# Attention with two mixtures of experts: score products of both halves of a tile in a row, and gate products between the transposes and the products with v

## The chip, the cores and the metric

One core of a Trainium2 chip runs the whole kernel. The metric is the device time of one execution in microseconds (us). TensorE is called PE in the profile, VectorE DVE, ScalarE ACT, GpSimd POOL and SyncE SP.

## The reference

Attention over 4 batches, 8 heads, 576 positions and 64 columns a head, with a window of 128 positions and a distance bias; then a mixture of 8 experts (one per token, by the largest gate logit), then a dense mixture of 4 experts weighted by given probabilities.

```python
scores = scale * np.matmul(q, k.transpose(0, 1, 3, 2))
mask = (rel >= 0) & (rel < window)
scores = np.where(mask, scores + bias[None], -1000000000.0)
scores = scores - np.max(scores, axis=-1, keepdims=True)
attn = np.exp(scores)
attn = attn / (np.sum(attn, axis=-1, keepdims=True) + 1e-09)
x = np.matmul(attn, v)
...
expert_idx = np.argmax(x @ w_gate, axis=1)
out[mask] = gate_w[mask, None] * (np.maximum(x[mask] @ w1[e], 0.0) @ w2[e])
...
out += p[:, e:e + 1] * (np.maximum(x @ w1[e], 0.0) @ w2[e])
```

## The kernel before

The 2304 tokens are cut into 18 tiles of 128. A tile's queries see at most two tiles of keys (its own and the one before). Each tile is worked on in two halves of four heads; a half is a step `s`, so that tile `t` has the steps `2t` and `2t+1`, 36 in all. Only the attention part, the function `attention`, is touched by the change. The two mixtures come behind it, in `moe`.

One step of attention goes through these functions:

- `st_qk(s)`: TensorE writes the scores of a half into PSUM (tile `sc`). Two bf16 products with the identity bring the bias in (L375), then twelve products of q and k follow (L383). q and k are each split into an upper and a lower part, and the heads come in pairs, each head on 64 of the 128 rows.
- `st_max(s)`: VectorE takes the negative maximum of each row (L392, tile `nm`).
- `st_exp(s, jj)`: ScalarE takes the exponentials of one pair of heads (L400, tile `pr`), two instructions a call.
- `st_pv_t(s, jj)`: TensorE transposes the probabilities of a pair (L411, tile `pt` in PSUM), and ScalarE copies them to SBUF (L413, tile `ptr`).
- `st_pv(s)`: TensorE multiplies them with v (L426, tile `xo`). The rows of `vr` hold v, a one for the row's sum, and eight columns with the gate products of v, so that `xo` gives the gate logits too.
- `st_row(s)`: VectorE divides by the row's sum (L442 to L450); with the second half the logits of the tile are summed (L471).
- `st_vw(t)`: TensorE makes the gate products of v for one tile (L462, tile `vw`), and VectorE copies them into `vr` (L463).

The order in which the loop at L572 writes these calls is the order on each engine's queue, as each engine takes its instructions in the order of the program. Before, step `s` writes the scores of `s`, its maximum and half of its exponentials, the products with v of `s-2`, in odd steps the gate products of the tile, then the transposes of `s-1` around the other half of the exponentials of `s`. Behind these stand the chores: the splits of k and q for later tiles on VectorE (`split_k`, `split_q`), loads, in six steps the split of a weight tile (`w_split`: upper part on ScalarE at L126, lower part on VectorE at L130, one step later), and small pieces of the routing (`route_op`). At the start `busy` gives TensorE products of zeros that nobody reads (L97).

PSUM holds two buffers of `sc`, two of `pt`, and two (pool `ps_m`) that `xo`, `vw` and the routing's counts take in turn. `pr` has two buffers in SBUF.

Of the kernel before, what the change touches and what calls it, by code (L numbers as in the profile page):

```python
# [9 lines left out]
F32 = mybir.dt.float32  # L10
# [7 lines left out]
P = 128  # L18
# [29 lines left out]
def kernel(  # L48
# [44 lines left out]
    def busy(pool, tag, n):  # L93

        ps = pool.tile([P, DM], F32, tag=tag, name="idle")
        for _ in range(n):
            nc.tensor.matmul(ps, idle[:, 0:P], idle, start=True, stop=True)  # L97
# [69 lines left out]
    def attention():  # L167
        actx = ExitStack()
        with actx:
# [32 lines left out]
            def split_k(t):  # L202
                rk = raw_k.pop(t)
                c = t % NSLOT
                nc.vector.tensor_copy(out=khi[:, :, c, :], in_=rk)
                nc.vector.tensor_tensor(
                    out=klo[:, :, c, :], in0=rk, in1=khi[:, :, c, :].bitcast(F32), op=ALU.subtract
                )

            def split_q(t):  # L210
                rq = raw_q.pop(t)
                hi = qpool.tile([P, NP, P], F32R, tag="qhi", name=f"qhi{t}")
                lo = qpool.tile([P, NP, P], F32R, tag="qlo", name=f"qlo{t}")
                nc.vector.tensor_scalar(out=hi, in0=rq, scalar1=0.125, scalar2=None, op0=ALU.mult)
                nc.vector.scalar_tensor_tensor(
                    out=lo, in0=rq, scalar=0.125, in1=hi.bitcast(F32), op0=ALU.mult, op1=ALU.subtract
                )
                qs[t] = hi, lo
# [139 lines left out]
            def geom(t):  # L358
                cur, prv = t % NSLOT, (t - 1) % NSLOT
                if t in opens:  # L360
                    return [t], slice(cur, cur + 1), P
                if prv < cur:
                    return [t - 1, t], slice(prv, cur + 1, cur - prv), 0
                return [t, t - 1], slice(cur, prv + 1, prv - cur), P

            def st_qk(s):
                t, hf = divmod(s, 2)
                keys, sl, b0 = geom(t)
                w = len(keys) * P
                bias = biases[1 if t in split_tiles else 2 if t - 1 in split_tiles else 0]  # L370
                qhi, qlo = qs[t]
                ps = ps_s.tile([P, 2, 2, 2 * P], F32, tag="sc", name=f"sc{s}")
                for r in range(2):
                    h = 4 * hf + r
                    nc.tensor.matmul(  # L375
                        ps[:, r, :, 0:w], identb, bias[:, h:h + 3:2, b0:b0 + w], start=True, stop=False
                    )
                for jj in range(2):
                    j = 2 * hf + jj
                    for x, (ql, kl) in enumerate(((qhi, khi), (qhi, klo), (qlo, khi))):  # L380
                        for r in range(2):
                            rows = slice(r * D, (r + 1) * D)
                            nc.tensor.matmul(  # L383
                                ps[:, r, jj, 0:w], ql[rows, j, :], kl[rows, j, sl, :],
                                start=False, stop=(jj == 1 and x == 2),
                            )
                sc[s] = ps

            def st_max(s):
                w = len(geom(s // 2)[0]) * P  # L390
                nm = small.tile([P, 2, 2], F32, tag="nm", name=f"nm{s}")
                nc.vector.tensor_reduce(out=nm, in_=sc[s][:, :, :, 0:w], axis=AX.X, op=ALU.max, negate=True)  # L392
                pr = spool.tile([P, 2, 2, 2 * P], F32, tag="pr", name=f"pr{s}")
                prob[s] = pr, nm

            def st_exp(s, jj):
                w = len(geom(s // 2)[0]) * P
                pr, nm = prob[s]
                for r in range(2):
                    nc.scalar.activation(  # L400
                        out=pr[:, r, jj, 0:w], in_=sc[s][:, r, jj, 0:w], func=AF.Exp,
                        bias=nm[:, r, jj:jj + 1], scale=1.0,
                    )
# [12 lines left out]
            def st_pv(s):  # L416
                t, hf = divmod(s, 2)
                keys = geom(t)[0]
                nk = len(keys)
                xo = ps_m.tile([P, 4, D + 1 + E1], F32, tag="m", name=f"xo{s}")  # L420
                for jj in range(2):
                    pt = probt.pop((s, jj))
                    for r in range(2):
                        h = 4 * hf + 2 * jj + r
                        for c in range(nk):
                            nc.tensor.matmul(  # L426
                                xo[:, 2 * jj + r, :], pt[:, r, c, :], vr[:, keys[c] % NSLOT, h, :],
                                start=(c == 0), stop=(c == nk - 1),
                            )
                xos[s] = xo  # L430
# [5 lines left out]
            def st_row(s):  # L436
                t, hf = divmod(s, 2)
                xo = xos.pop(s)
                if hf == 0:
                    rowt[t] = xpool.tile([P, H, D], F32, tag="row", name=f"xrow{t}", bufs=7)  # L440
                den = small.tile([P, 4, 1], F32, tag="den", name=f"den{s}")
                nc.vector.tensor_scalar(out=den, in0=xo[:, :, D:D + 1], scalar1=1e-9, scalar2=None, op0=ALU.add)  # L442
                nc.vector.reciprocal(out=den, in_=den)
                nc.vector.tensor_tensor(
                    out=rowt[t][:, 4 * hf:4 * hf + 4, :], in0=xo[:, :, 0:D],
                    in1=den.to_broadcast([P, 4, D]), op=ALU.mult,
                )
                if hf == 0:
                    lgh[t] = xpool.tile([P, H, E1], F32, tag="lgh", name=f"lgh{t}")
                nc.vector.tensor_tensor(  # L450
                    out=lgh[t][:, 4 * hf:4 * hf + 4, :], in0=xo[:, :, D + 1:],
                    in1=den.to_broadcast([P, 4, E1]), op=ALU.mult,
                )
                if hf == 1:
                    st_logits(t)
# [111 lines left out]
            def route_op():  # L567
                todo = gates if gates and (not back or gates[0][0] < back[0][0]) else back
                if todo and next(todo[0][1], True):
                    todo.pop(0)  # L570

            for s in range(ns + 2):  # L572
                t, hf = divmod(s, 2)
                if s == 2:
                    split_k(1)
                    split_q(1)
                    busy(ps_t, "t", 3)
                if s < ns:
                    st_qk(s)
                    if s == 1:  # L580
                        busy(ps_t, "t", 4)
                    st_max(s)
                    st_exp(s, 0)
                route_op()
                if 2 <= s < ns + 2:
                    st_pv(s - 2)
                    st_row(s - 2)
                if hf == 1 and s < ns:
                    st_vw(t)
                    if t + 2 < NTT:  # L590
                        load_v(t + 2)
                route_op()
                if 1 <= s < ns + 1:
                    st_pv_t(s - 1, 0)
                if s < ns:
                    st_exp(s, 1)
                if 1 <= s < ns + 1:
                    st_pv_t(s - 1, 1)
                if s < ns:
                    if hf == 0:  # L600
                        if 2 <= t + 1 < NTT:
                            split_k(t + 1)
                        if t + 3 < NTT:
                            load(t + 3)
                    elif t + 2 < NTT:
                        split_q(t + 2)
                    if s == 1:
                        row_consts()
                    if s in (3, 5):
                        w_dma(nxt["dma"])  # L610
                    if s < E1:
                        clear_rows(s)
                    if s == 20:
                        domain_probs()
                    for _ in range(5):
                        if next(consts, True):
                            pass
                route_op()
                if late:
                    late.pop(0)()  # L620
                if s in SPLITS:
                    w_split(late)
                route_op()
            while late:
                late.pop(0)()
            for todo in (back, gates):
# [583 lines left out]
```

## Time and profile before

| What | Value |
|---|---|
| median of 3 runs | 1202.87 us (1201.73 to 1203.39) |
| the profiled execution's own time | 1197.88 us |
| its span in the trace | 1196.2 us |
| mean granted TensorE clock | 0.993 |
| PE busy | 1167.6 us, 98% |
| DVE busy | 785.6 us, 66% |
| ACT busy | 517.7 us, 43% |
| POOL busy | 94.7 us, 8% |

The shares are averages over stages with different limits. Attention takes roughly the first 176 us of the span. A busy TensorE in these tables is one whose matmul records cover the time; matmul records overlap, so the pace is read from the starts of successive records, not from their lengths.

### The profile page before, as it was taken

How to read it: one execution, taken by the hardware profiler on the slowest of the kernel's cores; microseconds unless marked ns; L12 is line 12 of the kernel's file. 1: busy time of each engine (PE TensorE's matmuls, PEld its weight loads, DVE VectorE, ACT ScalarE, POOL GpSimd, SP SyncE). 2: the span in 40 equal slices, each digit the busy share in tenths (PEclk: the TensorE clock that was granted, in tenths of full speed). 3: DMA queues.
4: the chain of work that ended last, by engine and by line, in shares of the span. 5: the costliest groups of instructions: out<-in, count | busy, mean ns of one | idle time of the engine just before them, and what ended most of it. 6: DMA issues, size and time to landing. Idle time of an engine off the chain costs nothing.

```text
span 1196.2 us, 18240 instructions
## 1 busy us (share of the span) xinstructions
PE 1167.6 (98%) x7006; PEld 1061.4 (89%) x7006; DVE 785.6 (66%) x1434; ACT 517.7 (43%) x926; POOL 94.7 (8%) x127
## 2 busy tenths in 40 slices
PE   8999998999999999999999899999999999999997
PEld 6888877999999988999999799999998899999996
DVE  6878764555565467666667876666667766666663
ACT  4565542454454344333334444443334433333331
POOL 8300110012200000000000110000000200000001
PEclk9999999999999999999999999999999999999999
DMA  9755424464574322222222222222221322222201
GB/s 315 262 163 188 142 63 155 143 200 141 159 221 149 124 72 71 71 71 71 65 63 67 89 88 69 57 69 71 71 65 58 124 72 71 71 71 71 71 19 53
DMA packets 62232, 126.67 MB, mean 106 GB/s; under 512 B 26272, under 2 KB 26272, under 8 KB 62112
## 3 DMA queue, kind: packets, MB, share of 16 engines
q1 hardware_dynamic: 58368, 114.96, 30.7%
q0 software_dynamic: 3456, 9.51, 2.1%
q8 instruction: 83, 1.36, 0.5%
q10 hardware_dynamic: 288, 0.52, 0.1%
q14 instruction: 37, 0.30, 0.1%
HBM read 109.18 MB, written 15.80 MB: 104 GB/s over the span
## 4 chain that ended last, share of the span: by engine, by line
issue 42%; PE 37%; DVE 2%; POOL 2%; ACT 1%; POOLq 0%; ACTq 0%; DVEq 0%
PE g L679 10%; PE l L1120 9%; PE y L786 8%; PE X L1026 4%; PE Z L1026 2%; POOL out_dram L1141 2%; PE y L797 1%; PE Y L1026 1%; PE xps L742 1%; DVE hlo L1062 1%; DVE x L701 0%; ACT hhi L1057 0%; DVE x L1056 0%; ACT whi L126 0%; PE g L767 0%
## 5 line engine op out<-in xcount | busy, mean ns | idle before, releaser
L130 DVE TENSOR_TENSOR wlo<-raw,whi 128x1024 fp32r<-128x1024 f32 x160 | 195.0, 1221 | 113.4 <-ACT whi L126 113.3
L1120 PE MATMUL l<-whi,hhi 128*128 128x512 f32 x576 | 225.4, 391 | 4.3 <-DVE acc L1137 4.0
L126 ACT CAST whi<-raw 128x1024 fp32r<-128x1024 f32 x160 | 168.3, 1057 | 134.1 <-DVE raw L152 104.6
L1120 PE MATMUL l<-whi,hlo 128*128 128x512 f32 x576 | 225.6, 392 | 0.0
L1120 PE MATMUL l<-wlo,hhi 128*128 128x512 f32 x576 | 225.3, 391 | 0.0
L1047 ACT COPY x<-X 128x384 f32<-128x384 f32 x138 | 65.8, 480 | 237.7 <-PE X L1026 237.7
L1137 DVE SCALAR_TENSOR_TENSOR acc<-l,ct,acc 128x512 f32<-128x512 f32 x126 | 94.3, 749 | 82.2 <-PE l L1120 82.2
L1120 PEld LDWEIGHTS l<-whi,hhi 128*128 128x128 f32 x576 | 108.6, 189 | 27.5 <-DVE acc L1137 4.8
L1120 PEld LDWEIGHTS l<-whi,hlo 128*128 128x128 f32 x576 | 108.5, 188 | 22.9 <-DVE hlo L1062 0.3
L1120 PEld LDWEIGHTS l<-wlo,hhi 128*128 128x128 f32 x576 | 108.6, 189 | 22.0
L1057 ACT ACTIVATE hhi<-x 128x384 fp32r<-128x384 f32 x144 | 74.1, 526 | 75.0 <-DVE x L1056 75.0
L1056 DVE TENSOR_TENSOR x<-Z,x 128x384 f32<-128x384 f32 x92 | 50.8, 556 | 81.9 <-ACT x L1047 72.9
L1141 POOL DMA_INDIRECT out_dram<-acc,ctok x18 | 23.0, 1276 | 842.9 <-DVE acc L1137 493.2
L1062 DVE SCALAR_TENSOR_TENSOR hlo<-x,hhi 128x384 fp32r<-128x384 f32 x144 | 77.4, 554 | 11.5 <-ACT hhi L1057 7.5
L400 ACT ACTIVATE pr<-sc,nm 128x256 f32<-128x256 f32 (+1 forms) x144 | 58.9, 464 | 52.4 <-DVE nm L392 24.6
L426 PE MATMUL xo<-vr,ptr 128*128 128x73 f32 x544 | 69.0, 279 | 0.6 <-ACT ptr L413 0.5
L786 PE MATMUL y<-hhi,whi 128*128 128x256 f32 (+2 forms) x224 | 69.5, 310 | 0.0
L786 PE MATMUL y<-hhi,wlo 128*128 128x256 f32 (+2 forms) x224 | 69.1, 308 | 0.0
L786 PE MATMUL y<-hlo,whi 128*128 128x256 f32 (+2 forms) x224 | 68.9, 308 | 0.0
L426 PEld LDWEIGHTS xo<-vr,ptr 128*128 128x128 f32 x544 | 63.7, 192 | 5.8 <-ACT ptr L413 1.3
L667 DVE SCALAR_TENSOR_TENSOR hlo<-g,hhi 128x384 fp32r<-128x384 f32 x64 | 32.7, 552 | 29.8 <-ACT hhi L666 29.5
L666 ACT ACTIVATE hhi<-g 128x384 fp32r<-128x384 f32 x64 | 28.0, 489 | 54.5 <-PE g L767 41.7
(337 smaller groups left out, 2546.4 us busy)
## 6 DMA issues: line engine op xcount, KB each, us to landing
raw<-in_w_b_dram SPq DMA_DIRECT2D x96, 512.0 KB, 3.5
raw<-in_w_a_dram SPq DMA_DIRECT2D x64, 512.0 KB, 4.1
xs<-zrow SPq DMA_DIRECT2D x8, 768.0 KB, 6.9
row<-xs SPq DMA_DIRECT2D x7, 768.0 KB, 5.6
rk<-in_k_dram SPq DMA_DIRECT2D x18, 256.0 KB, 4.9
vr<-in_v_dram SPq DMA_DIRECT2D x18, 256.0 KB, 3.9
rv<-in_vt_dram SPq DMA_DIRECT2D x18, 256.0 KB, 3.4
rq<-in_q_dram SPq DMA_DIRECT2D x16, 256.0 KB, 5.2
```

What stands on the lines that cost most here:

```text
L126: nc.scalar.copy(out=hi, in_=src)
L130: nc.vector.tensor_tensor(out=lo, in0=src, in1=hi.bitcast(F32), op=ALU.subtract)
L400: nc.scalar.activation(out=pr[:, r, jj, 0:w], in_=sc[s][:, r, jj, 0:w], func=AF.Exp, bias=nm[:, r, jj:jj + 1], scale=1.0,)
L426: nc.tensor.matmul(xo[:, 2 * jj + r, :], pt[:, r, c, :], vr[:, keys[c] % NSLOT, h, :], start=(c == 0), stop=(c == nk - 1),)
L679: nc.tensor.matmul(ps[:, 0:w], wl[:, c0:c0 + P], xl[dt // 2][:, dt % 2, 0:w], start=(n == 0), stop=(n == 3 * NDT - 1),)
L786: nc.tensor.matmul(acc[:, 0:w], wl[:, c0:c0 + P], hl[:, 0:w], start=(f == 0 and x == 0), stop=(f == NFT - 1 and x == 2),)
L1026: nc.tensor.matmul(ps, wl[:, c0 + kt * P:c0 + (kt + 1) * P], xl[:, kt, :], start=(start and kt == 0 and x == 0), stop=(kt == 1 and x == 2) ...
L1047: nc.scalar.copy(out=to, in_=xb[i])
L1057: nc.scalar.activation(out=hi, in_=c, func=AF.Relu)
L1062: nc.vector.scalar_tensor_tensor(out=lo, in0=c, scalar=0.0, in1=hi.bitcast(F32), op0=ALU.max, op1=ALU.subtract)
L1120: nc.tensor.matmul(acc, hl[:, ts], wl[:, c0:c0 + DM], start=(m == 0 and x == 0), stop=(m == 3 and x == 2),)
L1137: nc.vector.scalar_tensor_tensor(out=accs[g], in0=acc, scalar=pe, in1=accs[g], op0=ALU.mult, op1=ALU.add)
```

## The change

The loop runs over tiles instead of steps. For a tile, the scores of both halves are written one behind the other, each with its maximum, then all exponentials of the first half. Then come the products with v of the first half of the tile before, the transposes of its second half, the chores of the even step, all exponentials of the second half, the gate products, the products with v of the second half of the tile before, the transposes of this tile's first half, and the chores of the odd step. The buffer of `pr` is taken when the first exponential is written, not with the maximum. In the first tile the gate products stand ahead of four of the products of zeros instead of behind them.

```diff
                 nm = small.tile([P, 2, 2], F32, tag="nm", name=f"nm{s}")
                 nc.vector.tensor_reduce(out=nm, in_=sc[s][:, :, :, 0:w], axis=AX.X, op=ALU.max, negate=True)
-                pr = spool.tile([P, 2, 2, 2 * P], F32, tag="pr", name=f"pr{s}")
-                prob[s] = pr, nm
+                prob[s] = nm
 
             def st_exp(s, jj):
                 w = len(geom(s // 2)[0]) * P
+                if jj == 0:
+                    prob[s] = spool.tile([P, 2, 2, 2 * P], F32, tag="pr", name=f"pr{s}"), prob[s]
                 pr, nm = prob[s]
...
-            for s in range(ns + 2):
+            def chores(s):
                 t, hf = divmod(s, 2)
-                if s == 2:
-                    split_k(1)
-                    split_q(1)
-                    busy(ps_t, "t", 3)
-                if s < ns:
-                    st_qk(s)
-                    if s == 1:
-                        busy(ps_t, "t", 4)
-                    st_max(s)
-                    st_exp(s, 0)
-                route_op()
-                if 2 <= s < ns + 2:
-                    st_pv(s - 2)
-                    st_row(s - 2)
-                if hf == 1 and s < ns:
-                    st_vw(t)
-                    if t + 2 < NTT:
-                        load_v(t + 2)
-                route_op()
-                if 1 <= s < ns + 1:
-                    st_pv_t(s - 1, 0)
-                if s < ns:
-                    st_exp(s, 1)
-                if 1 <= s < ns + 1:
-                    st_pv_t(s - 1, 1)
...
+            for t in range(NTT + 1):
+                s = 2 * t
+                if t == 1:
+                    split_k(1)
+                    split_q(1)
+                    busy(ps_t, "t", 3)
+                if t < NTT:
+                    for n in (s, s + 1):
+                        st_qk(n)
+                        st_max(n)
+                    for jj in range(2):
+                        st_exp(s, jj)
+                route_op()
+                if t > 0:
+                    st_pv(s - 2)
+                    st_row(s - 2)
+                    route_op()
+                    for jj in range(2):
+                        st_pv_t(s - 1, jj)
+                chores(s)
+                if t < NTT:
+                    for jj in range(2):
+                        st_exp(s + 1, jj)
+                    st_vw(t)
+                    if t == 0:
+                        busy(ps_t, "t", 4)
+                route_op()
+                if t > 0:
+                    st_pv(s - 1)
+                    st_row(s - 1)
+                if t + 2 < NTT:
+                    load_v(t + 2)
+                route_op()
+                if t < NTT:
+                    for jj in range(2):
+                        st_pv_t(s, jj)
+                chores(s + 1)
```

**TensorE in tile 11** (steps 22 and 23). The numbers in the names are steps for `sc`, `xo`, `pt` and `ptr`, and tiles for `vw`. Before, the first half's scores are followed by products with v:

```order
L383 MATMUL sc22_1679<-khi_116,qlo11_1532 128x256 x2
L426 MATMUL xo20_1700<-vr_118,ptr20_0_1659 128x73 x4
L426 MATMUL xo20_1700<-vr_118,ptr20_1_1668 128x73 x4
L411 MATMUL pt21_0_1717<-ident_68,pr21_1629 128x128 x4
L411 MATMUL pt21_1_1726<-ident_68,pr21_1629 128x128 x4
L375 LDWEIGHTS identb_168
L375 MATMUL sc23_1742<-bias0_171,identb_168 128x512
```

and the second half's scores too, with the gate products behind them:

```order
L383 MATMUL sc23_1742<-khi_116,qlo11_1532 128x256 x2
L426 MATMUL xo21_1762<-vr_118,ptr21_0_1722 128x73 x4
L426 MATMUL xo21_1762<-vr_118,ptr21_1_1731 128x73 x4
L462 MATMUL vw11_1777<-wbd_189,rv11_1511 128x16 x4
L411 MATMUL pt22_0_1786<-ident_68,pr22_1696 128x128 x4
L411 MATMUL pt22_1_1795<-ident_68,pr22_1696 128x128 x4
L375 LDWEIGHTS identb_168
```

Now, behind the second half's scores of the same tile:

```order
L383 MATMUL sc23_1696<-khi_116,qlo11_1532 128x256 x2
L427 MATMUL xo20_1719<-vr_118,ptr20_0_1661 128x73 x4
L427 MATMUL xo20_1719<-vr_118,ptr20_1_1668 128x73 x4
L412 MATMUL pt21_0_1736<-ident_68,pr21_1629 128x128 x4
L412 MATMUL pt21_1_1743<-ident_68,pr21_1629 128x128 x4
L463 MATMUL vw11_1764<-wbd_189,rv11_1513 128x16 x4
L427 MATMUL xo21_1770<-vr_118,ptr21_0_1741 128x73 x4
L427 MATMUL xo21_1770<-vr_118,ptr21_1_1748 128x73 x4
L412 MATMUL pt22_0_1788<-ident_68,pr22_1713 128x128 x4
L412 MATMUL pt22_1_1795<-ident_68,pr22_1713 128x128 x4
```

The scores of step 23 have moved ahead of `xo20`, and `vw11` now stands between the transposes `pt21` and the products `xo21` that read them.

**ScalarE near the end of attention** (steps 30 to 32). Before, two exponentials stand between the copies of a step's two pairs:

```order
L400 ACTIVATE pr30_2237<-sc30_2220,nm30_2235 128x256 x2
L413 COPY ptr29_0_2263<-pt29_0_2258 128x512
L400 ACTIVATE pr30_2237<-sc30_2220,nm30_2235 128x256 x2
L413 COPY ptr29_1_2272<-pt29_1_2267 128x512
L400 ACTIVATE pr31_2307<-sc31_2290,nm31_2305 128x256 x2
L413 COPY ptr30_0_2341<-pt30_0_2336 128x512
```

Now:

```order
L401 ACTIVATE pr30_2254<-sc30_2220,nm30_2235 128x256 x4
L414 COPY ptr29_0_2282<-pt29_0_2277 128x512
L414 COPY ptr29_1_2289<-pt29_1_2284 128x512
L401 ACTIVATE pr31_2307<-sc31_2237,nm31_2252 128x256 x4
L414 COPY ptr30_0_2343<-pt30_0_2338 128x512
L414 COPY ptr30_1_2350<-pt30_1_2345 128x512
```

All four exponentials of a step now stand ahead of the first copy, and the two copies follow each other.

## Rows read from the trace of the kernel before

**Rows 1.** Busy time of each engine in one stretch, most of attention; last: PEclk, DMA share, GB/s

```profile
22.00:163.00 141.00, 139.84 (x1297) 122.33 (x1296) 112.75 (x315) 85.06 (x196) 30.00 (x50) 1.00 0.59 188
```

**Rows 2.** Waits of PE in that stretch: us in total, times, longest

```profile
PE rkp L513 <- DVE oh_all L506: 0.8, 1, 0.8
```

**Rows 3.** Timeline of PE, tile 11: start, us, line, count [idle before]

```profile
103.75 0.59 PE L375 MATMUL sc<-bias,identb 128*128 128x512 bf16 x2
...
105.19 2.01 PE L426 MATMUL xo<-vr,ptr 128*128 128x73 f32 x16
107.03 1.04 PE L411 MATMUL pt<-ident,pr 128*128 128x128 f32 x8
107.90 0.59 PE L375 MATMUL sc<-bias,identb 128*128 128x512 bf16 x2
...
109.33 2.01 PE L426 MATMUL xo<-vr,ptr 128*128 128x73 f32 x16
111.17 1.01 PE L462 MATMUL vw<-wbd,rv 128*128 128x16 f32 x8
112.03 1.07 PE L411 MATMUL pt<-ident,pr 128*128 128x128 f32 x8
112.94 0.59 PE L375 MATMUL sc<-bias,identb 128*128 128x512 bf16 x2
```

**Rows 4.** Timeline of PE, the last five of the sixteen products from 105.19

```profile
106.47 0.72 PE L426 MATMUL xo<-vr,ptr 128*128 128x73 f32 x5
```

**Rows 5.** Timeline of DVE, tiles 11 and 12

```profile
107.98 0.18 DVE L450 TENSOR_TENSOR lgh<-xo,den 128x32 f32<-128x32 f32 x1
...
109.20 1.22 DVE L130 TENSOR_TENSOR wlo<-raw,whi 128x1024 fp32r<-128x1024 f32 x1
...
112.74 0.42 DVE L214 TENSOR_SCALAR qhi<-rq 128x512 fp32r<-128x512 f32 x1
113.19 0.69 DVE L215 SCALAR_TENSOR_TENSOR qlo<-rq,qhi 128x512 fp32r<-128x512 f32 x1
114.48 1.23 DVE L392 TENSOR_REDUCE nm<-sc 128x4 f32<-128x1024 f32 x1 [0.60 <-PE sc L383]
```

**Rows 6.** Timeline of ACT, tiles 11 and 12

```profile
112.70 0.58 ACT L413 COPY ptr<-pt 128x512 f32<-128x512 f32 x1 [0.22 <-PE pt L411]
...
115.80 0.47 ACT L400 ACTIVATE pr<-sc,nm 128x256 f32<-128x256 f32 x1 [1.30 <-DVE nm L392]
```

**Rows 7.** Timeline of PE, the end of attention

```profile
169.89 2.33 PE L426 MATMUL xo<-vr,ptr 128*128 128x73 f32 x16 [0.24 <-ACT ptr L413]
172.06 1.04 PE L411 MATMUL pt<-ident,pr 128*128 128x128 f32 x8
```

**Rows 8.** Timeline of ACT, the end of attention

```profile
169.26 0.58 ACT L413 COPY ptr<-pt 128x512 f32<-128x512 f32 x1 [1.10 <-PE pt L411]
169.74 0.84 ACT L400 ACTIVATE pr<-sc,nm 128x256 f32<-128x256 f32 x2
170.46 0.60 ACT L413 COPY ptr<-pt 128x512 f32<-128x512 f32 x1
...
172.75 1.07 ACT L413 COPY ptr<-pt 128x512 f32<-128x512 f32 x2 [1.58 <-PE pt L411]
```

**Rows 9.** Timeline of DVE, the start, steps 1 and 2

```profile
10.50 0.23 DVE L463 COPY vr<-vw 128x64 f32<-128x64 f32 x1 [1.07 <-PE vw L462]
10.80 0.43 DVE L214 TENSOR_SCALAR qhi<-rq 128x512 fp32r<-128x512 f32 x1
```

**Rows 10.** Loads of q issued from 6.4 to 9 us: first and last issue, and landing

```profile
L191 SPq DMA_DIRECT2D rq<-in_q_dram x2: 376/404/431, 6.5 to 7.5; - x2
...
DMA to landing us min/median/max: 4.3/4.4/4.5
```

**Rows 11.** Timeline of PE, the start, first product of q and k of step 2

```profile
13.70 0.39 PE L383 MATMUL sc<-khi,qhi 64*128 64x256 f32 x2 [1.28 <-DVE qhi L214]
```

**Rows 12.** Busy time of each engine in one stretch at the start (columns as in Rows 1)

```profile
15.00:21.00 6.00, 6.00 (x44) 4.78 (x41) 4.56 (x10) 2.39 (x7) 5.78 (x9) 0.72 1.07 388
```

## The prediction

> **What bounds the kernel now.** I read first the busy time of a stretch that holds most of attention. [...] Second, the waits of TensorE in it: one of 0.8 us, for the routing, and no other [rows 2]. So TensorE's own order of work sets the pace, and no maximum, exponential or copy is waited for. Third, the timeline of TensorE over one tile, to see what each piece takes from its start to the next one's: scores of the first half 105.19 - 103.75 = 1.44 us, products with v 1.84, transposes 0.87, scores of the second half 1.43, products with v 1.84, gate products 0.86, transposes 0.91, together 9.19 us [rows 3]. The pieces touch each other. A reorder can therefore win only what it costs to go over from one kind of product to another, and what is lost at the two ends of attention, where TensorE does wait.
>
> **The cost of going over.** The sixteen products with v behind a score piece take 1.84 us [rows 3]. Their last five take 107.03 - 106.47 = 0.56, so 0.112 each [rows 3, 4]; sixteen at that pace are 1.79. The first one behind the scores thus costs 0.05 us more. The gate products and the transposes behind them take 0.86 + 0.91 = 1.77; eight gate products at 0.112 and the transposes as they are behind products with v (0.87) would be 1.77 too [rows 3, 4]. Going from v to gate to transposes costs nothing.
>
> **The change, part by part.**
>
> *Scores in a row.* No product is added or removed. Per tile one passage from scores to products with v goes (-0.05), and one from scores to the bias product of the next scores comes. The trace has no such passage at full width; its bounds are nothing, as behind transposes, and 0.05, as for products with v. I take nothing: the bias product is the only one here with a bf16 identity as its weights, like those behind the transposes in the row at 107.90. 17 tiles have products with v in them (the first has none): 17 x 0.05 = **-0.9 us**, bounds -0.9 and 0.
>
> *Gate products between transposes and products with v.* The passages from transposes to gate and from gate to v are new, that from v to gate is gone. Nearest rows: 0 (v, gate, transposes) and 0.05 each (scores to v). I take 0, as the same three kinds of fp32 products stand there; the upper end would be 17 x 0.1 = +1.7.
>
> *What covers the copies.* Products with v of the second half read copies of transposes that now stand only the gate products (0.86) ahead, where 1.43 of scores stood before; and all four exponentials stand ahead of these copies. Counted from the tile's start: scores 1.44 + 1.43 = 2.87, products with v to 4.71, transposes to 5.58, gate products to 6.44. The maximum starts 114.48 - 112.94 = 1.54 after a tile's start when VectorE is free [rows 3, 5], the exponentials 2.86 after it [rows 3, 6]. Two take 0.84 [rows 8], so four are done by 4.54. The first copy starts 112.70 - 112.03 = 0.67 behind the start of its transposes [rows 3, 6], at 5.38, and is done at 5.96; a pair of copies takes 1.07 [rows 8], to 6.45. Needed are 6.44 and, eight products later, 7.34. So the first copy has 0.48 us to spare, the exponentials another 5.38 - 4.54 = 0.84: the maximum may come 1.3 us late before TensorE notices. Cost: **0**; what it costs without that cover is a rival.
>
> *PSUM.* The second half's `xo` now takes the buffer of the first half's. `st_row` leaves it 108.16 - 107.03 = 1.13 us behind the end of its products [rows 3, 5]: at 4.71 + 1.13 = 5.84, ahead of 6.44. Cost 0.
>
> *Scores ahead of time, loads, splits.* The second half's scores need the exponentials of the tile before out of their buffer; those end behind the copies at 6.45 by about 8.1 (four at 0.42), or 9.2 where a weight's upper split comes between, against 9.14 + 1.44. The load of v for a later tile is issued some 0.7 us later in its tile, two tiles ahead of its use. Cost 0.
>
> *The end.* In the last tile the products with v of step 34 take 172.06 - 169.89 = 2.17 us instead of 1.84, as two exponentials stand between the copies they need: the second copy ends at 171.06, while eight products from 169.89 are done at 170.79 [rows 7, 8]. Now the copies follow each other and are done 1.07 behind 169.26, at 170.33: **-0.3 us**. The waits for a first copy, ahead of this and of the last products, stay. The routing that follows hangs on these products, so the gain passes on; the bounds are -0.3 and 0.
>
> *The start.* The gate products of tile 0 stand ahead of four products of zeros now, so VectorE's copy at 10.50 comes sooner. Behind it stands the upper part of q at 10.80 [rows 9], and its load lands 4.3 to 4.5 us behind its issue at 6.5, at 10.8 to 11.0 [rows 10]. So that part still starts at 10.8, and TensorE's wait until 13.70 stays [rows 11]: 0. Behind it TensorE has the same work in another order.
>
> The sum is -0.9 - 0.3 = -1.2 us. Against the profiled execution's own 1197.88 us that is 1196.7. That execution lies 5.0 us under the median of the runs shown, so I put the difference on the median: 1202.87 - 1.2 = **1201.7 us**.
>
> [...] The row shows the extra 0.05 us where the first weights for v come behind the scores [rows 3, 4]. [...]
>
> **The rivals.**
>
> *A: the passage moves.* The 0.05 us belong to any change of kind and come back between scores and bias, or between transposes, gate and v. For it: each piece behind the scores in the trace is paid for. Against: v to gate to transposes is free. Worked out from the bounds above: one 0.05 back gives -0.3, 1202.6; two more give +1.4, 1204.3; I set it at 1203.0. [...]
>
> *B: slower, VectorE late for the maximum.* The maximum of the first half stands behind `st_row` of the last half and the split of q (0.42 + 0.69). `st_row` now ends about 0.26 us into a tile (its products end 0.87 ahead of it, plus 1.13), the logits' sum and the split at about 1.6: already the 1.54 at which the maximum could start. With four routing pieces of 0.18 (as the row at 107.98) and a lower split of 1.22 [rows 5] it comes 0.1 + 0.7 + 1.2 = 2.0 late. It decides from 1.3 on. There are six weight splits: 6 x 0.7 = +4.2, hence 1205.9. Against it: VectorE has 141.00 - 112.75 us free [rows 1], and three of the six stand in the even step, behind both maxima.
>
> [...]
>
> **How the numbers follow.** The forecast has 0.61, A 0.16, B 0.09, C 0.14. A measurement of this kernel tells about 0.2% (2.4 us) from no change, so faster means under 1200.5 and slower over 1205.3. C gives faster nearly always, the forecast now and then (its runs spread over 1.7 us): faster 0.18. B and the far end of A give slower: 0.1. The rest is the same: 0.72. The range reaches from a little under C, 1199.4, to the far end of A and a little more, 1204.8; it leaves out B and some of C.
>
> **What would show it.** A tile of about 9.14 us instead of 9.19 from bias product to bias product; products with v behind the gate products taking 1.79 and those behind scores 1.84; no wait of TensorE for a copy from 22 to 163 us; the products of step 34 at about 1.8. A is right if the gate products or the bias products behind scores have grown by 0.05. B shows as waits of the products with v for L414. C shows as a clock of 1.00 from 15 to 21 us. The forecast is wrong if attention's steady tiles are longer than 9.2 us, or if the time moves by more than 2.4 us for something that no tile shows.

## The result, and the profile after

| What | Before | After |
|---|---|---|
| median | 1201.46 us (6 runs, 1197.73 to 1203.39) | 1210.56 us (6 runs, 1208.55 to 1211.25) |
| the profiled execution's own time | 1197.88 us | 1208.55 us |
| its span | 1196.2 us | 1206.8 us |
| mean granted TensorE clock in it | 0.993 | 0.988 |

The changed kernel is slower: ratio 1.0074, 95% interval 1.0057 to 1.0092. The forecast was 1201.7 us with a range up to 1204.8, so the time is 8.9 us over the forecast and outside the range: the forecast was a gain of 1.2 us, measured is a loss of 9.1.

**The plain tile got shorter.** Timeline of TensorE after, one tile without routing counts (start, duration, engine, line; [idle before]), which answers to [rows 3]:

```profile
62.11 0.59 PE L375 MATMUL sc<-bias,identb 128*128 128x512 bf16 x2
...
63.55 0.61 PE L375 MATMUL sc<-bias,identb 128*128 128x512 bf16 x2
...
64.98 2.01 PE L427 MATMUL xo<-vr,ptr 128*128 128x73 f32 x16
66.82 1.04 PE L412 MATMUL pt<-ident,pr 128*128 128x128 f32 x8
67.69 0.96 PE L463 MATMUL vw<-wbd,rv 128*128 128x16 f32 x8
68.51 1.99 PE L427 MATMUL xo<-vr,ptr 128*128 128x73 f32 x16
70.33 1.04 PE L412 MATMUL pt<-ident,pr 128*128 128x128 f32 x8
71.20 0.59 PE L375 MATMUL sc<-bias,identb 128*128 128x512 bf16 x2
```

From start to start: scores 1.44 and 1.43, products with v 1.84, transposes 0.87, gate products 0.82, products with v 1.82, transposes 0.87: 9.09 us where it was 9.19. The attention stage as a whole got longer all the same. Busy time of each engine in four stretches (columns as in [rows 1]); the second line answers to [rows 1], the first to [rows 12]:

```profile
15.00:21.00 6.00, 6.00 (x57) 5.17 (x54) 5.25 (x13) 3.95 (x11) 5.65 (x9) 1.00 1.07 383
22.00:163.00 141.00, 136.04 (x1212) 118.38 (x1208) 106.04 (x294) 77.90 (x182) 28.05 (x49) 0.95 0.58 185
...
47.27:54.10 6.83, 6.83 (x34) 5.93 (x35) 2.43 (x9) 1.41 (x4) 3.04 (x3) 0.50 0.63 201
...
105.30:112.13 6.83, 5.72 (x28) 4.74 (x29) 4.03 (x18) 2.68 (x6) 2.92 (x3) 0.50 0.73 195
```

TensorE is covered for 136.04 us of 141.00 instead of 139.84, and its granted clock there is 0.95 instead of 1.00: two stretches of 6.83 us ran at 0.50. The waits of TensorE from 22 to 163 us (us in total, times, longest) answer to [rows 2]:

```profile
PE xo L427 <- DVE vr L464: 2.7, 5, 1.1
PE rkp L514 <- DVE oh_all L507: 1.9, 2, 1.4
```

There were 0.8 us of waits before, there are 4.6 now. Both lines are the routing's. The first is new.

**Where the 8 us sit.** The length of each tile, from its first bias product (L375) to the next tile's, in both traces. Five groups of tiles end at tile 2, 5, 8, 11 and 13, and their routing's counts (`rkp`) come two tiles later, in tiles 4, 7, 10, 13 and 15:

| Tiles | Before | After | Difference |
|---|---|---|---|
| 2, 3, 6, 8, 9, 12, 14, 16 (no counts) | 72.44 us | 71.76 us | -0.68 |
| 4 and 5 | 18.88 | 23.11 | +4.23 |
| 10 and 11 | 17.33 | 21.72 | +4.39 |
| 7, 13 and 15 | 29.03 | 30.63 | +1.60 |

Together +9.54. Ahead of them, the bias product of tile 2 starts 1.35 us earlier (20.81 us for 22.16); behind them the products of step 34 take 1.85 us, from

```profile
178.15 2.01 PE L427 MATMUL xo<-vr,ptr 128*128 128x73 f32 x16 [0.29 <-ACT ptr L414]
180.00 0.71 PE L412 MATMUL pt<-ident,pr 128*128 128x128 f32 x5
```

where they took 2.17 [rows 7]. 9.54 - 1.35 - 0.3 = 7.9 us, and these transposes do start 180.00 - 172.06 = 7.94 later. So the counts cost 10.2 us in five tiles (with the tiles 5 and 11 behind them), and the rest of attention is 2.3 us shorter, 1.35 of it at the start, where the clock has a part (below). The other 2.7 us by which the two profiled executions differ lie behind these transposes, most of it the mixtures, whose code is the same.

**What happens in a tile with counts.** Tile 4 on TensorE before, a part of the tile:

```profile
44.68 0.31 PE L509 MATMUL rkp<-base,top 128*128 128x32 f32 x2
45.09 0.18 PE L513 MATMUL rkp<-oh_all,tri 128*128 128x32 bf16 x1
45.11 0.22 PE L515 MATMUL rkp<-oh_all,ones 128*128 128x24 bf16 x3
45.19 0.59 PE L375 MATMUL sc<-bias,identb 128*128 128x512 bf16 x2
```

and after:

```profile
44.60 0.31 PE L510 MATMUL rkp<-base,top 128*128 128x32 f32 x2
45.49 0.18 PE L514 MATMUL rkp<-oh_all,tri 128*128 128x32 bf16 x1 [0.59 <-DVE oh_all L507]
45.52 0.22 PE L516 MATMUL rkp<-oh_all,ones 128*128 128x24 bf16 x3
45.60 1.04 PE L463 MATMUL vw<-wbd,rv 128*128 128x16 f32 x8
47.10 1.16 PE L427 MATMUL xo<-vr,ptr 128*128 128x73 f32 x5 [0.47 <-DVE vr L464]
```

VectorE after, over the same time:

```profile
40.85 1.22 DVE L130 TENSOR_TENSOR wlo<-raw,whi 128x1024 fp32r<-128x1024 f32 x1
41.98 0.18 DVE L503 TENSOR_TENSOR key<-key,kc 128x24 f32<-128x24 f32 x1
42.08 2.35 DVE L392 TENSOR_REDUCE nm<-sc 128x4 f32<-128x1024 f32 x2
...
45.26 0.17 DVE L507 TENSOR_TENSOR oh_all<-key,km 128x24 bf16<-128x24 f32 x1
45.35 0.42 DVE L205 CAST khi<-rk 128x512 fp32r<-128x512 f32 x1
45.81 0.69 DVE L206 TENSOR_TENSOR klo<-rk,khi 128x512 fp32r<-128x512 f32 x1
46.42 0.18 DVE L520 TENSOR_TENSOR rk<-rkp,oh_all 128x24 f32<-128x24 f32 x1
...
46.80 0.16 DVE L523 COPY base<-rkp 128x8 f32<-128x8 f32 x1
46.87 0.21 DVE L464 COPY vr<-vw 128x64 f32<-128x64 f32 x1
```

Two maxima (2.35 us) now stand in a row ahead of `oh_all`, which the counts need: first wait. Then come the counts (`rkp`), the gate products (`vw`) and `xo7`. All three take buffers of the pool `ps_m`, which has two, so `xo7` takes the counts' buffer back. Its last reader is the copy of `base` (L523), behind the split of k (L205, L206): second wait. The profile names the later `vr<-vw` at L464 as the releaser, but that copy feeds later products: in the plain tile above, the products with v start at 68.51, ahead of it.

```profile
70.06 0.22 DVE L464 COPY vr<-vw 128x64 f32<-128x64 f32 x1
```

What frees the buffer is L523, ending 0.14 us before `xo7` starts. Before, 1.43 us of scores stood between the counts and the next `xo`. Tile 10 has the same two waits, longer: tile 9 sees only one tile of keys and so gives less cover (its two score pieces take 1.13 and 1.14 us from start to start, not 1.44 and 1.43), and the sums of the domain probabilities (L345 to L348, 105.42 to 106.41 us on VectorE) stand ahead of the copy of `base` too:

```profile
104.49 0.18 PE L514 MATMUL rkp<-oh_all,tri 128*128 128x32 bf16 x1 [1.36 <-DVE oh_all L507]
...
106.94 1.96 PE L427 MATMUL xo<-vr,ptr 128*128 128x73 f32 x8 [1.11 <-DVE vr L464]
```

Tile 17 has counts too, but no further tile whose k is split. There `base` is copied in time, and the products with v follow the gate products without a wait:

```profile
174.12 1.04 PE L463 MATMUL vw<-wbd,rv 128*128 128x16 f32 x8
175.00 1.99 PE L427 MATMUL xo<-vr,ptr 128*128 128x73 f32 x16
```

```profile
174.56 0.15 DVE L523 COPY base<-rkp 128x8 f32<-128x8 f32 x1
```

Three theories went to the chip. **P**: the routing's chain on VectorE has lost its slack, above all through the counts' PSUM buffer; its form **I** adds that the idle time is what lets the clock fall. **S**: scores in a row alone make VectorE late (rival B). **D**: the denser order itself takes the clock down.

### The profile page after: what moved, and what is told of

It is laid out like the page before. It is cut to its first block, busy times and chain, and to the rows that moved or that the text cites. A ratio compares the mean times of both kernels' runs of the same rounds, so it can differ in the third digit from the quotient of the medians.

```text
span 1206.8 us, 18267 instructions
## 1 busy us (share of the span) xinstructions
PE 1173.8 (97%) x7006; PEld 1067.3 (88%) x7006; DVE 786.1 (65%) x1434; ACT 516.8 (43%) x926; POOL 92.7 (8%) x127
## 4 chain that ended last, share of the span: by engine, by line
issue 41%; PE 38%; POOL 2%; DVE 1%; ACT 1%; POOLq 0%; ACTq 0%; DVEq 0%
PE g L693 10%; PE l L1134 9%; PE y L800 8%; PE X L1040 5%; PE Z L1040 2%; POOL out_dram L1155 2%; PE y L811 1%; PE Y L1040 1%; PE xps L756 1%; DVE x L715 0%; DVE hlo L1076 0%; ACT whi L126 0%; PE g L781 0%; ACT t2h L710 0%; ACT hhi L1071 0%
## 5 line engine op out<-in xcount | busy, mean ns | idle before, releaser
L401 ACT ACTIVATE pr<-sc,nm 128x256 f32<-128x256 f32 (+1 forms) x144 | 55.1, 475 | 43.4 <-DVE nm L392 43.4
L414 ACT COPY ptr<-pt 128x512 f32<-128x512 f32 (+1 forms) x72 | 37.4, 569 | 36.6 <-PE pt L412 36.4
```

What stands on the lines that cost most here:

```text
L401: nc.scalar.activation(out=pr[:, r, jj, 0:w], in_=sc[s][:, r, jj, 0:w], func=AF.Exp, bias=nm[:, r, jj:jj + 1], scale=1.0,)
```

## The experiments

In the first four the kernel before had a median of 1202.09 us (27 runs), in the next four 1202.02 (16), in the last three 1201.98 (24).

**First: read the counts earlier.** The changed kernel, with two routing steps ahead of the split of k in even steps instead of behind it.

```diff
             def chores(s):
                 t, hf = divmod(s, 2)
+                for _ in range(2 - 2 * hf):
+                    route_op()
...
-                route_op()
+                if hf == 1:
+                    route_op()
```

(and the same `if` ahead of the last one).

> The changed kernel, with the two routing pieces of the even step ahead of the split of k, so that VectorE reads the counts out of PSUM before it splits k. Theory P (the PSUM buffer of the counts): in the tiles with counts the products with v of the second half wait for the counts' buffer, and VectorE frees it only behind the split of k. Then these waits (2.7 us in 5 places in the changed kernel) go; the waits of the counts for the one-hot (1.9 us in 2) stay; the clock stays at its upper level in at least one of the two places where it fell. Time 1201 to 1205 us. Theory S (the scores in a row alone make VectorE late, the counts' buffer does not matter): the time stays at 1209 to 1211.

Measured: 1202.53 us, ratio 1.0011 (0.9993 to 1.0028). The wait for `xo` is gone, that for `oh_all` as long as ever, and the clock is 1.00:

```profile
PE rkp L514 <- DVE oh_all L507: 1.9, 2, 1.4
```

```profile
22.00:163.00 141.00, 138.77 (x1299) 121.19 (x1298) 113.25 (x316) 83.21 (x195) 27.74 (x49) 1.00 0.59 186
```

Eight of nine us come back for routing steps moved ahead of the splits of k; in the tiles with counts these are three small instructions (L520, L522 and L523). P holds. D falls, and S as the main cause, as the scores still stand in a row and the order of TensorE is unchanged. What may be left of S is the wait for `oh_all`.

**Second: counts ahead of the tile's first products with v.** The four routing steps of a tile's chores now all stand in the odd step, two instead of one stand ahead of the first products with v, and three weight splits move one step on. So the counts stand behind the second half's scores.

```diff
-SPLITS = 6, 11, 16, 21, 26, 31
+SPLITS = 7, 11, 17, 21, 27, 31
...
                     for jj in range(2):
                         st_exp(s, jj)
-                route_op()
+                for _ in range(2):
+                    route_op()
...
-                route_op()
+                for _ in range(4 * hf if s < ns else 0):
+                    route_op()
```

(The `route_op` calls ahead of `late` and behind the gate products go.)

> The changed kernel, with the counts' products between the scores of the second half and the first products with v, all pieces of the routing that lead to them ahead of the tile's first maximum, and the weight splits begun in odd steps (7, 11, 17, 21, 27, 31), so that their lower part stands behind the maxima. Theory P: the counts then find the one-hot done and their buffer is read two pieces ahead of its next use; TensorE has no wait over 0.1 us from 22 to 176 us, the clock stays at its upper level there, and the gain per tile (9.09 us instead of 9.19) is left: 2 to 4 us under the kernel before, 1197 to 1200. Theory S: scores in a row stay slower, 1207 or more. Theory D (the denser order itself makes the clock fall): the clock falls twice as in the changed kernel, 1206 or more.

Measured: 1199.81 us, ratio 0.9983 (0.9973 to 0.9993): faster than both kernels. One wait of 1.0 us is left from 22 to 163 us, where none over 0.1 was expected, at a clock of 1.00.

**Third: fill the idle time.** The changed kernel with products of zeros ahead of the counts and of the gate products in tiles 4 and 10; they add work that nobody reads.

```diff
+                for _ in range({0: 5, 2: 11}.get(g, 0)):
+                    nc.tensor.matmul(full, idle[:, 0:P], idle[:, 0:4 * (D + 1 + E1)], start=True, stop=True)
...
+                for _ in range({4: 5, 10: 10}.get(t, 0)):
+                    nc.tensor.matmul(full, idle[:, 0:P], idle[:, 0:4 * (D + 1 + E1)], start=True, stop=True)
```

> The changed kernel, with products of zeros that nobody reads where TensorE waits in tiles 4 and 10: 5 and 11 of 292 columns ahead of the counts, 5 and 10 ahead of the gate products. The order of the work and the waits for VectorE stay. Theory I (it is TensorE's idle time in these two tiles that takes the clock down): the granted clock is 1.00 from 22 to 176 us, and about 6.8 us come back, 1203 to 1205 us. Theory D (the denser order or the load as such takes it down): the clock falls at both places as before, and the time is 1210 to 1212.

Measured: 1206.05 us, ratio 1.0026 (1.0009 to 1.0042). The time lies between the two expectations. In its profile the clock stays up in tiles 4, 5, 10 and 11, and falls instead behind two later, unfilled waits, in tiles 13 and 15, each time for 3.4 us. In tile 13:

```profile
132.10 1.98 PE L427 MATMUL xo<-vr,ptr 128*128 128x73 f32 x16 [0.39 <-DVE vr L467]
133.91 1.74 PE L412 MATMUL pt<-ident,pr 128*128 128x128 f32 x8
135.44 1.06 PE L375 MATMUL sc<-bias,identb 128*128 128x512 bf16 x2
```

(the transposes take 1.53 us to the next start instead of 0.87). Filling cannot bring the lateness back, so I take the 4.5 us that came back in the median for the clock's. This profiled execution (1207.48 us) shows only a part of them: the products of step 34 start 1.6 us earlier than in the changed kernel. That the clock stays up where the idle time is filled supports I.

**Fourth: the gate products back behind the products with v**, so the first part of the change without the second.

```diff
                         st_exp(s + 1, jj)
-                    st_vw(t)
...
                     st_row(s - 1)
+                if t < NTT:
+                    st_vw(t)
```

> The changed kernel with the gate products back behind the products with v of the second half: the scores in a row are the only part left of the change. Theory P: the products with v no longer wait for the counts' buffer, but they follow right behind the transposes whose copies they read, and wait for these copies 0.4 to 0.5 us in nearly every tile, some 7 us in all; 1203 to 1212 us by how often the clock falls. Theory S: slower too, with waits for the one-hot of 1.9 us and the clock falling at the same two places, 1209 to 1212, and no waits for copies.

Measured: 1209.72 us, ratio 1.0054 (1.0038 to 1.0069). TensorE now waits for copies of the transposes:

```profile
PE xo L427 <- ACT ptr L414: 3.0, 9, 0.6
PE vw L463 <- issue: 1.2, 1, 1.2
PE rkp L514 <- DVE oh_all L507: 0.8, 1, 0.8
```

So with the scores in a row the gate products must cover these copies, as the prediction had it, though the waits are 3.0 us and not some 7. The wait of 1.2 us, in tile 10, is one for the counts' buffer again: in this order `vw` takes it, and the copy of `base` ends 0.11 us ahead of `vw`.

**Fifth: the second part alone**, on the kernel before.

```diff
                 route_op()
+                if hf == 1 and s < ns:
+                    st_vw(t)
                 if 2 <= s < ns + 2:
                     st_pv(s - 2)
                     st_row(s - 2)
                 if hf == 1 and s < ns:
-                    st_vw(t)
```

> The kernel before with the second part of the change alone: in odd steps the gate products stand ahead of the products with v, behind the scores; the scores keep their old places. P (the counts' PSUM buffer is the cause): the products with v behind the gate products take the counts' buffer here too, but a whole scores piece (1.44 us) lies between, so the base copy (46.4 us in the first tile with counts of the kernel before) is long done when they start (about 47.5): no wait for vr, clock 1.00 through attention, time as before, ratio 0.999 to 1.002. D (the gate products between other pieces lower the clock or cost at each passage): 18 x 0.05 = +0.9 us at least, and with falls of the clock 3.4 or 6.8 more, ratio over 1.003. S (scores in a row are the cause): as before too, ratio 0.999 to 1.002.

Measured: 1207.94 us, ratio 1.0051 (1.0034 to 1.0068). P as I had put it was wrong here: there is no wait for `vr`, but the waits for `oh_all` are longer than in the change. TensorE in tile 10:

```profile
100.35 0.31 PE L509 MATMUL rkp<-base,top 128*128 128x32 f32 x2
102.33 0.18 PE L513 MATMUL rkp<-oh_all,tri 128*128 128x32 bf16 x1 [1.67 <-DVE oh_all L506]
```

The gate products now stand ahead of the second half's `xo`, so the logits of a tile come a gate piece (0.86 us [rows 3]) later, and with them, as I read it, the chain of routing steps behind: key, maximum, `oh_all`, counts. P was widened: each part takes slack from that chain.

**Sixth: three weight splits one step on**, nothing else (`SPLITS` as in the second).

> The changed kernel with three of the six weight splits one step later, so that their lower parts on VectorE (1.22 us each) no longer stand ahead of the two maxima of tiles 4, 9 and 14. S (VectorE late for two maxima in a row is the cause): the maxima of these tiles are 1.2 us earlier and half of the loss comes back, about 1206, and with the fall at 47 us 3.4 more: 1203 to 1206. P: in tile 4 the lower part now stands between the two routing steps, ahead of the copy of base, so the wait for oh (0.59) goes and the wait for vr grows by as much, from 0.47 to about 1.1; tile 10 (1.36 and 1.11) is as it was; time 1206.5 to 1210.5, the lower end if one wait of 1.1 in tile 4 does not take the clock down where two of 0.59 and 0.47 did.

Measured: 1209.05 us, ratio 1.0069 (1.0042 to 1.0096). As P had it, the lower split moved from ahead of the maxima to ahead of the copy of `base`, and the wait with it; S falls. In tile 4 it is one wait now:

```profile
48.63 1.10 PE L427 MATMUL xo<-vr,ptr 128*128 128x73 f32 x4 [1.39 <-DVE vr L464]
```

and the clock falls there all the same (from 48.14 us on). So two waits close together are not needed for a fall.

**Seventh: the second experiment with the sums of the domain probabilities one tile later.**

```diff
-                    if s == 20:
+                    if s == 22:
```

> The second experiment (counts ahead of the second half's products with v, odd splits) with the sums of the domain probabilities one tile later (step 22 instead of 20, a tile without counts). P: the one wait of 1.0 us that was left there (gate products in tile 10) goes: 1199.8 - 1.0 = 1198.8, ratio 0.996 to 0.999, clock 1.00 from 20 to 170 us, no wait over 0.4 us. S: nothing to gain here either; as the second experiment at best, ratio 0.998. D: no statement on it, as the order is the same.

Measured: 1200.06 us, ratio 0.9972 (0.9946 to 0.9998): as fast as the second, but the wait did not go, so its cause was not the sums. TensorE, and VectorE at the same time:

```profile
104.49 1.03 PE L463 MATMUL vw<-wbd,rv 128*128 128x16 f32 x8 [1.01 <-PE pt L412]
```

```profile
104.23 0.15 DVE L523 COPY base<-rkp 128x8 f32<-128x8 f32 x1
```

The transposes named had long ended. The copy of `base` ends 0.11 us ahead: with the counts ahead of `xo18` it is `vw` that takes their buffer. The two maxima stand ahead of that copy, and tile 10 has short cover, as tile 9 sees one tile of keys only. The same buffer, in one tile of five.

**Eighth: one routing step between the two maxima**, so that `oh_all` comes sooner.

```diff
                         st_max(n)
+                        if n == s:
+                            route_op()
...
                     st_row(s - 2)
-                    route_op()
```

> The changed kernel with one routing step moved from behind the first half's products with v to between the two maxima: oh_all comes about 0.66 us earlier, and the copy of base stays where it is, behind the splits of k. So TensorE idles as long in all in each tile with counts, but in one piece instead of two: in tile 4 about 0 for oh and 1.1 for vr (was 0.59 and 0.47), in tile 10 about 0.7 and 1.8 (was 1.36 and 1.11). P with the clock following the idle time in all: falls at 47 and 105 us as in the changed kernel, 1208 to 1211. P with the clock following two waits close behind each other: no fall at 47, and perhaps none at 105: 1203 to 1207. S: oh_all is not late any more in tile 4, so its part of the loss comes back and the waits for vr should shrink too: 1204 to 1206 with waits for vr under 0.5.

Measured: 1209.53 us, ratio 1.0065 (1.0045 to 1.0085). The experiment missed its aim, as the wait for `oh_all` in tile 4 was replaced by another for a buffer of `ps_m`: `vw` takes that of `xo6`, whose reading by `st_row` now stands behind `oh_all`.

```profile
46.36 1.03 PE L463 MATMUL vw<-wbd,rv 128*128 128x16 f32 x8 [0.55 <-PE rkp L516]
47.92 1.90 PE L427 MATMUL xo<-vr,ptr 128*128 128x73 f32 x10 [0.52 <-DVE vr L464]
```

TensorE waits 4.9 us in all (4.6 in the change), and the clock falls in the same two places, as P expected for a clock that follows the idle time. An earlier `oh_all` alone buys nothing here; S expected 1204 to 1206.

**Ninth to eleventh: the counts of the first three groups a tile later.** One edit, made to the fifth experiment (ninth), to the first (tenth) and to the changed kernel (eleventh):

```diff
                 yield
+                for _ in range(8 if g < 3 else 0):
+                    yield
                 pr = ps_m.tile([P, m + 1, E1], F32, tag="m", name=f"rkp{g}")
```

A tile has eight `route_op` calls, so the counts keep their place in the tile, but `oh_all` is long written.

> The fifth experiment (the kernel before with the gate products ahead of the products with v) with the routing of the first three groups held for one tile between oh_all and the counts: the counts stand at the same place of the step, a tile later, when oh_all has long been written. P, as widened by the fifth experiment (each part takes slack from the routing's chain on VectorE, which TensorE waits for in tiles with counts): the waits for oh_all (0.9 and 1.7 us) go, and with them the fall of the clock at 102 us; 1207.9 goes back to 1201 to 1203.5. D (the place of the gate products itself costs): waits gone, but time still over 1205, with falls of the clock at places without a wait.

> The first experiment (the changed kernel with the copy of base ahead of the splits of k) with the routing of the first three groups held for one tile between oh_all and the counts, as in the ninth. Neither wait is left: no wait for oh_all or vr from 20 to 170 us, clock 1.00 there. P: 1202.5 - 2 = about 1200.5 (1199 to 1201.5), a little faster than before. S or D: no better than the first experiment, 1202.5 or more.

> The changed kernel with the routing of the first three groups held for one tile between oh_all and the counts, and nothing else: the wait for oh_all goes, the wait for the copy of base stays (base is still copied behind the splits of k). P: waits for vr of 0.3 to 1.2 us in three tiles, none for oh_all before 130 us; half or more of the loss comes back, 1203 to 1208, the upper end if the clock still falls behind the waits for base. If the PSUM buffer is harmless and only oh_all counts: 1200 to 1202.5, as the tenth.

Measured, ninth: 1201.79 us, ratio 0.9989 (0.9971 to 1.0006), with no wait for `oh_all` from 22 to 163 us and a clock of 1.00. So the second part alone costs nothing once the routing has its slack back. Tenth: 1199.93 us, ratio 0.9983 (0.9964 to 1.0002), the clock 1.00. Its expectation of no wait was not quite met; one of 0.7 us remains, in tile 10:

```profile
PE xo L427 <- DVE oh_all L507: 0.7, 1, 0.7
```

Here `xo19` takes the buffer of `xo18`, which `st_row` reads only behind the two maxima (its last reading ends at 100.02 us, `xo19` starts at 100.17). So a little of S is there.

Eleventh: 1209.05 us, ratio 1.0066 (1.004 to 1.0091), a little over the end of its range; the half or more of the loss that should have come back did not. The waits for `oh_all` are gone, those for the counts' buffer are 3.1 us instead of 2.7, the longest in tile 11, where the lower split of a weight now stands ahead of the copy. In tile 5, TensorE and the reader on VectorE:

```profile
54.13 1.04 PE L463 MATMUL vw<-wbd,rv 128*128 128x16 f32 x8
55.69 2.50 PE L427 MATMUL xo<-vr,ptr 128*128 128x73 f32 x16 [0.52 <-DVE vr L464]
```

```profile
55.39 0.15 DVE L525 COPY base<-rkp 128x8 f32<-128x8 f32 x1
```

With the first experiment these make a table of two by two:

| | wait for the copy of `base` | no wait for it |
|---|---|---|
| wait for `oh_all` | the change, 1.0074 | first, 1.0011 |
| no wait for it (first three groups) | eleventh, 1.0066 | tenth, 0.9983 |

Taking away the wait for the buffer is worth 0.6 to 0.8%. Taking away that for `oh_all` gives 0.1 to 0.3%, which the intervals do not tell from nothing.

**The clock against the waits.** From 22 to 163 us, one profiled execution each:

| Kernel | Waits of TensorE, us | Granted clock |
|---|---|---|
| before | 0.8 | 1.00 |
| ninth, tenth | 0.6, 0.7 | 1.00, 1.00 |
| second, seventh | 1.0, 1.0 | 1.00, 0.97 (0.99 from 27.1 us on) |
| third | 1.3 | 0.98 |
| first | 1.9 | 1.00 |
| fifth | 2.6 | 0.96 |
| eleventh | 3.1 | 0.90 |
| the change, sixth, eighth | 4.6, 4.6, 4.9 | 0.95, 0.95, 0.95 |
| fourth | 5.0 | 0.97 (0.99 from 26.5 us on) |

In the fourth and the seventh a fall that began before 22 us, ahead of all these waits, reaches into the stretch. The eleventh's profiled execution was the slowest of its seven (1218.58 us).

## Why the prediction was wrong

**PSUM, "Cost 0": the step that failed.** The prediction looked at who had `xo`'s buffer in a plain tile, found the first half's `xo` there, and worked out rightly that it is free in time. In the tiles with counts these stand between, so the buffer is theirs, and in five of them its last reader hangs behind the splits of k. The kernel's description itself says that `xo`, `vw` and the counts take these buffers in turn. The waits this made are 2.7 us in five, and by the two-by-two table the term is worth 0.63 to 0.83%, 7.6 to 10 us, with the clock that follows them.

**"What it costs without that cover" was priced for the wrong thing.** The prediction asked when the copies would be late, and found 1.3 us to spare; from 22 to 163 us no copy of a transpose is waited for, so that was right. What lost its cover was the wait of [rows 2], 0.8 us before, 1.9 now. It was read as a single event, not as a chain with no slack left, and no term was made for it.

**The clock was held constant.** Two falls of 6.83 us to 0.50 cost, worked out from the granted clock, 3.4 us and (6.83 - 1.11) / 2 = 2.9 us, the second less because TensorE idled for 1.11 us of it. That is 6.3 of the 10.2 us that the tiles with counts cost, more than the waits.

**Scores in a row, -0.05 a tile: right in sign, from another place.** The eight tiles without counts got 0.68 / 8 = 0.085 shorter. In the tile shown, products with v behind scores still take 1.84 and those behind gate products 1.82 rather than 1.79, so only 0.02 is from there; the gate products (0.82 for 0.86) and the transposes at the tile's end (0.87 for 0.91) gave 0.04 each. So going from v to gate to transposes was not free: the prediction priced the gate products at the 0.112 of products with v, but behind transposes eight of them take 0.82. The gate term, 0 with bounds 0 to +1.7, was a gain.

**The end, -0.3:** right (1.85 for 2.17). **The start, 0:** the fourth step's bias product came 1.35 us sooner. The granted clock from 15 to 21 us is 1.00 for 0.72 [rows 12], as rival C had it, though it fell earlier instead, to 0.50 from 9.73 to 13.1 us. The new order does not settle that: in the fourth and the seventh experiment, which have it too, the clock from 15 to 21 us is 0.59 and 0.65, and in the ninth, with the old order of the scores, 1.00.

**The rivals.** A did not happen: neither the gate products nor the bias products behind scores grew. C stood for a clock of 1.00 instead of 0.72 from 15 to 21 us, an estimated 6 x 0.28 = 1.7 us by [rows 12], so for 1201.7 - 1.7 = 1200.0 us. Its sign was there, and 1.35 of the 1.7 came; but by the runs above that was the chance of this execution. B is the nearest: VectorE late, two maxima and a weight split ahead, slower. But it named the copies as what would be late, and the six weight splits as the occasions; it was the routing, in the five tiles with counts, and moving three splits (sixth) brought nothing back that the intervals show.

**What stays open.** Which wait takes the clock down is not settled. In one profiled execution each, a wait of 1.35 us for `oh_all` in the first experiment did not, one of 0.52 in the eleventh was followed by a fall, and the same wait of 1.0 was followed by one in the seventh but not in the second. How much of the loss is the wait for `oh_all` is open too (0.1 to 0.3%). And the 2.7 us by which the profiled executions differ behind attention were not followed up.

## What to carry to other kernels

Before a piece of TensorE work is moved, list every taker of its PSUM pool in every kind of tile, the rare ones too, with the last reader of each buffer and what stands ahead of that reader on its engine. A wait that is rare and short in the trace (here one of 0.8 us [rows 2]) can mark a chain without slack, and whatever the change puts ahead of that chain is a term of the sum. Where TensorE is almost always busy at the full clock, a new wait can cost more than its length: here 3.8 us of new waits came with lower clocks worth 6.3 us, though in the first experiment 1.9 us of waits cost no clock. Look first for a small read that can be moved ahead of longer work: here moving three brought eight of nine us back.

## What the hardware did that I had not expected

Idle time of 0.59 and 0.47 us in a stage that was otherwise covered was followed by 6.83 us at a granted clock of 0.50, which cost 3.4 us, three times its own length. A fall can also be much longer: in the eleventh's profile the clock stayed at 0.50 for 17 us, from 88.0 us on, while TensorE was covered all the time. And falls come where no experiment here looked: both kernels' profiles have them from the end of attention to 1190 us too, 10.2 us at 0.50 in all in each. Of the 67 runs of the kernel before beside the experiments, the fastest (1198.15 us) had a mean granted clock of 0.993 and the slowest (1212.20) one of 0.983; 0.010 of 1200 us would be 12 of these 14 us. Hence a change worth 0.1% can be seen in the tiles of one trace and not in the times.
